# Attention and Mish feed-forward in one fp32 kernel: first k and v over 128 partitions, q loads and result stores on two DMA queues, a new order of the beginning

## The chip, the cores and the metric

One core of one Trainium2 chip. The metric is the time of one execution on the device in microseconds (us). The kernel before was run three times; the median counts.

## The reference, cut to what matters

```python
# q, k, v: (8, 8, 576, 64) fp32 = (batch, heads, seq, head_dim); g_norm: (64,)
kv  = einsum('bhsd,bhse->bhde', k, v)
out = einsum('bhsd,bhde->bhse', q, kv)
out = out / sqrt(mean(out * out, axis=-1) + 1e-6) * g_norm
x   = out.transpose(0, 2, 1, 3).reshape(4608, 512)
# moe_w_in: (512, 2048), moe_w_out: (2048, 512), handed over as float64
h   = x @ w_in
g   = h * tanh(log1p(exp(h)))       # Mish
y   = g @ w_out                     # (4608, 512) fp32
```

## The kernel before, in words

The 4608 tokens are worked in nine blocks `j` of 512. Part 1 makes, for each block, the linear attention, the norm and the first matrix product with Mish, and stores `g` to DRAM (`gd`). Part 2 reads `g` back and makes the second matrix product, in 18 groups of 256 tokens.

Both matrix products use a seven-product scheme in the manner of Strassen (the forms A11, S1, S2, A12, S4, S3, A22 of the left side against T1 to T4, B11, B21, B22 of the weights). Each fp32 operand is split into two fp32r halves: ACT casts the high half (L117), VectorE (DVE) subtracts to get the low half (L118). So ACT and DVE pass work to and fro all the time. One product of a form is 12 matmuls in part 1 (`mm_in`, L489) and is called a slot; a block `j` has 28 slots, with its group of four times seven products. Sums of products are taken from PSUM by ACT copies (L452, L457, L466) and DVE adds (L510). A bank `a` or `bc` is written a second time only after ACT has copied it.

The weights come as float64 words. `weight_forms` loads a block (1 MB in two DMAs, L133), ACT scales it (L138), DVE joins the halves of the words (L143 to L145) and makes differences (L153 to L155), and ACT and DVE split the forms (L117, L118). There are eight such blocks for `w_in`, made between the start and about slot 15.

The order is written by hand: straight code from L548 to L593 for the beginning, then tables of steps by slot (`at(t, ...)`). Within each engine instructions run in this order. SP issues all loads and stores of part 1 up to the last block, in order. Every DMA carries one of eight semaphores that are handed out in turn, and its issue waits until the DMA that carried the same semaphore before it has landed; so SP has at most eight DMAs under way, and a ninth issue waits for the first.

The beginning: `weights(0, LOAD)` loads the first weight block; `kv_first` (L214) loads k and v of batch 0, four heads at a time, into 64 partitions of nine rows each, and `kv_first_product` (L223) multiplies them, 36 matmuls for two pairs of heads. A unit `u` (0 or 1) is four heads of a block. `load` (L288) of a unit fetches q for 32 partitions per DMA, four DMAs where the block lies in one batch and eight where it lies in two. `transpose` (L300, DVE), `project` (PE), `square` (ACT, L339 for the second unit of block 0), `sums` (PE), `rstd` (ACT: Ln and Exp, L370 and L371), `normalize` (DVE, L392) follow. In later blocks the row of `rstd` is stored to DRAM (`keep`, `rd`) and read back to all partitions (`spread`, L386). The q tile `qs` has one buffer, so the load of the next unit waits for the transpose of the one before. The load of unit 1 of a block stands at slot 3 (block 1) and later six slots before the block's end, just behind `spread`; that of unit 0 stands some nineteen slots before its block begins.

The store of results is `o_store` (L731): for each group of 256 tokens four DMAs of 32 partitions (more where the group crosses a batch). In the first group of part 2 it follows a chain of DVE adds (L832 to L838).

Of the kernel before, what the change touches and what calls it, by code (L numbers as in the profile page):

```python
# [26 lines left out]
def linear_attention_rms_mish_ffn(  # L27
# [33 lines left out]
    nc = tc.nc  # L61
# [62 lines left out]
    def weight_forms(srcs, m, n, room, forms, put=None):  # L124
# [4 lines left out]

        def load():  # L130
            t = room()
            for src, places in srcs:
                nc.sync.dma_start(t[:, places].rearrange("p b (m n) t -> p (b m) (n t)", m=m), src)  # L133
            st["w"] = t.rearrange("p b n t -> p (b n) t")
# [78 lines left out]

    def kv_first(h0):  # L214

        ts = []
        for src in (k, v):
            t = wfp.tile([S // 9, 4, 9 * D], F32, name="wf")
            nc.sync.dma_start(t, src[0, h0:h0 + 4].rearrange("h (p c) d -> p h (c d)", c=9))
            ts.append(t)  # L220
        return ts

    def kv_first_product(h0, kt, vt):  # L223
        for i in range(2):
            for c in range(9):
                for o in range(2):
                    d = slice(c * D, (c + 1) * D)
                    nc.tensor.matmul(kvps[o * D:(o + 1) * D, 0, h0 // 2 + i, :], kt[:, 2 * i + o, d], vt[:, 2 * i + o, d], start=(c == 0), stop=(c == 8))

# [55 lines left out]
    def unit_steps(j, u):  # L285
        st = {}

        def load(t=None):  # L288


            t = qs[u] = att.tile([P, 2, T // R * D], F32, name="qs") if t is None else t
            for i in range(4):
                for b, s0, cols in segments(j):
                    run = (cols.stop - cols.start) // R * D
                    src = q[b, 4 * u + i // 2, s0:s0 + 1, R * (i % 2):]
                    src = bass.AP(src.tensor, src.offset, [[run, R], [2 * S * D, 2], [1, run - R]])
                    c0 = cols.start // R * D
                    nc.sync.dma_start(t[i * R:(i + 1) * R, :, c0:c0 + run - R], src)

        def transpose():  # L300
            t = att.tile([P, 2, T], F32, name="fh" if j < T32 else "fl")
# [245 lines left out]

    nc.scalar.preload_act_table_set("natural_log_exp_and_others")  # L548
# [182 lines left out]
    def o_store(st):  # L731

        i, half = divmod(st["s"], T // G)
        for n in range(P // R):
            c = (half * G + n * R) // R
            for b, s0, cols in segments(i):
                first, L = cols.start // R, (cols.stop - cols.start) // R
                rs = [r for r in range(2) if first <= c + r * P // R < first + L]
                if rs:
                    row = b * S + s0 + c + rs[0] * P // R - first  # L740
                    dst = out[row:row + 1, :]
                    dst = bass.AP(dst.tensor, dst.offset, [[L * DM, R], [P // R * DM, len(rs)], [1, DM]])
                    nc.sync.dma_start(dst, st["o"][n * R:(n + 1) * R, rs[0]:rs[-1] + 1, :])

# [147 lines left out]
```

## Time and profile before

| what | value |
|---|---|
| three runs, median (lowest to highest) | 893.97 us (893.43 to 894.04) |
| the profiled execution's own time | 892.98 us |
| its span in the trace | 891.2 us |
| granted TensorE clock, mean over the span | 0.986 |
| PE busy / DVE busy / ACT busy | 829.7 / 614.2 / 460.8 us |

The profiled execution lies 0.99 us under the median of the runs. In rows of the timeline the columns are the start, the duration, the engine, the source line, the operation, the output and inputs, the shape, the count, and in brackets the idle time of the engine before it with what ended it. SPq and ACTq are rows in which SP or ACT issues a DMA.

### The profile page before, as it was taken

The numbers are of one execution on the slowest core, as the hardware profiler recorded it, in microseconds if no ns is written. First come the engines' busy times: TensorE is split into PE (matmuls) and PEld (weight loads), VectorE is DVE, ScalarE is ACT, GpSimd is POOL, SyncE is SP. The second block draws the span as 40 slices with busy tenths as digits, with TensorE's granted clock in tenths as the row PEclk, the third lists the DMA queues.
The fourth block names the chain that finished last, engine by engine and source line by source line (L and its number), as shares of the span: only waits on it lengthen the run. The fifth ranks groups of instructions, "written<-read, shape, count | busy, mean of one in ns | idle before, by whom it ended". The sixth has DMA issues, their size and how long they took to land.

```text
span 891.2 us, 17127 instructions
## 1 busy us (share of the span) xinstructions
PE 829.7 (93%) x7004; PEld 796.6 (89%) x7004; DVE 614.2 (69%) x808; ACT 460.8 (52%) x698; POOL 4.3 (0%) x21
## 2 busy tenths in 40 slices
PE   1678899998999999999999899999999999999997
PEld 1366699897999999999899899999999999999997
DVE  3799676776777667777765358876766667777772
ACT  2565666565575666666675344434444443434431
POOL 1000000000000000000000000000000000000000
PEclk9988999999999999999999999999999999999999
DMA  9958698987979897777567995344443443334421
GB/s 224 277 135 255 179 287 243 252 255 236 291 225 295 244 240 223 210 218 199 215 180 242 420 420 170 118 120 149 153 146 121 133 129 119 118 119 131 155 71 48
DMA packets 154766, 177.42 MB, mean 199 GB/s; under 512 B 17408, under 2 KB 135168, under 8 KB 153664
## 3 DMA queue, kind: packets, MB, share of 16 engines
q1 hardware_dynamic: 151936, 172.13, 64.0%
q10 hardware_dynamic: 2752, 4.20, 1.2%
q8 instruction: 55, 0.90, 0.4%
q14 instruction: 23, 0.19, 0.1%
HBM read 114.30 MB, written 62.00 MB: 198 GB/s over the span
## 4 chain that ended last, share of the span: by engine, by line
PE 65%; DMA 10%; DVE 10%; ACT 8%; issue 4%; SPq 1%; ACTq 0%; DVEq 0%
PE a L720 21%; PE bc L720 16%; PE a L489 14%; PE bc L489 8%; DMA gd<-ula 4%; PE s L246 2%; DVE ur L510 1%; DMA wf<-in_v_dram 1%; DMA gd<-ur 1%; DMA w<-in_moe_w_in_dram 1%; DMA vm<-in_v_dram 1%; DVE gf L118 1%; ACT L374 1%; ACT gf L117 1%; ACT L114 1%
## 5 line engine op out<-in xcount | busy, mean ns | idle before, releaser
L720 PE MATMUL a<-wf,gf 128*128 128x256 f32 x1632 | 201.8, 283 | 0.5 <-DVE ur L751 0.5
L720 PEld LDWEIGHTS a<-wf,gf 128*128 128x128 f32 x1632 | 198.4, 192 | 0.7 <-DVE ur L751 0.7
L118 DVE TENSOR_TENSOR gf<-g,gf 128x1024 fp32r<-128x1024 f32 (+1 forms) x123 | 133.0, 1087 | 89.4 <-ACT gf L117 89.4
L489 PE MATMUL a<-gf,wf 128*128 128x256 f32 x1296 | 175.3, 289 | 10.1 <-ACT ur L466 4.7
L489 PEld LDWEIGHTS a<-gf,wf 128*128 128x128 f32 x1296 | 165.6, 196 | 17.2 <-ACT ur L466 7.1
L489 PE MATMUL bc<-gf,wf 128*128 128x256 f32 x1296 | 170.7, 285 | 3.5 <-ACT ur L457 2.4
L489 PEld LDWEIGHTS bc<-gf,wf 128*128 128x128 f32 x1296 | 161.7, 191 | 5.1 <-ACT ur L457 2.6
L117 ACT CAST gf<-g 128x1024 fp32r<-128x1024 f32 (+1 forms) x123 | 114.5, 939 | 93.4 <-DVE g L700 65.1
L720 PE MATMUL bc<-wf,gf 128*128 128x256 f32 x1224 | 152.7, 283 | 1.3 <-DVE gf L118 1.3
L720 PEld LDWEIGHTS bc<-wf,gf 128*128 128x128 f32 x1224 | 149.4, 192 | 1.7 <-ACT gf L117 1.0
L489 PE MATMUL a<-a,wf 128*128 128x256 f32 x432 | 60.0, 290 | 7.1 <-DVE ur L510 7.1
L489 PEld LDWEIGHTS a<-a,wf 128*128 128x128 f32 x432 | 56.1, 195 | 10.3 <-DVE ur L510 5.2
L114 ACT ACTIVATE ur<-ur 128x1024 f32<-128x1024 f32 x36 | 38.1, 1059 | 38.5 <-DVE ur L510 38.5
L118 DVE TENSOR_TENSOR fa<-fl,fh 128x1024 fp32r<-128x1024 f32 x28 | 34.2, 1223 | 19.6 <-ACT fh L117 18.6
L118 DVE TENSOR_TENSOR gf<-gf 128x512 fp32r<-128x512 f32 x45 | 30.3, 689 | 23.0 <-ACT gf L117 23.0
L117 ACT CAST gf<-a 128x1024 fp32r<-128x1024 f32 x17 | 17.9, 1052 | 53.3 <-DVE a L697 50.8
L457 ACT COPY ur<-bc 128x512 f32<-128x512 f32 (+1 forms) x53 | 27.4, 517 | 31.7 <-PE bc L720 23.0
L117 ACT CAST gf<-gf 128x512 fp32r<-128x512 f32 x45 | 27.1, 618 | 31.8 <-DVE gf L413 19.1
L466 ACT COPY ur<-a 128x512 f32<-128x512 f32 (+1 forms) x53 | 27.4, 516 | 30.3 <-PE a L720 24.6
L510 DVE TENSOR_TENSOR ula<-bc,ula 128x512 f32<-128x512 f32 x36 | 24.7, 687 | 26.1 <-PE bc L489 26.0
L114 ACT ACTIVATE ula<-ula 128x512 f32<-128x512 f32 x36 | 22.8, 633 | 22.1 <-DVE ula L510 22.0
L510 DVE TENSOR_TENSOR ur<-bc,ur 128x512 f32<-128x512 f32 x36 | 24.4, 678 | 11.3 <-PE bc L489 5.7
(128 smaller groups left out, 850.2 us busy)
## 6 DMA issues: line engine op xcount, KB each, us to landing
g<-gd SPq DMA_DIRECT2D x18, 2048.0 KB, 8.7
gd<-ur SPq DMA_DIRECT2D x32, 512.0 KB, 3.4
wod<-wst SPq DMA_DIRECT2D x16, 896.0 KB, 5.9
wf<-wod SPq DMA_DIRECT2D x8, 1792.0 KB, 17.1
gd<-ula SPq DMA_DIRECT2D x32, 256.0 KB, 5.4
gd<-ulb SPq DMA_DIRECT2D x32, 256.0 KB, 4.8
w<-in_moe_w_out_dram SPq DMA_DIRECT2D x32, 256.0 KB, 5.0
km<-in_k_dram SPq DMA_DIRECT2D x28, 256.0 KB, 4.5
```

The costliest lines, as they stand in the source:

```text
L114: nc.scalar.activation(o, i, AF.Mish)
L117: nc.scalar.copy(hi, src)
L118: nc.vector.tensor_sub(lo, src, hi.bitcast(F32))
L246: nc.tensor.matmul(kvps[o * D:(o + 1) * D, b % 2, h0 // 2 + i, :], kt, vt, start=(c == 0), stop=(c == CM))
L374: nc.scalar.preload_act_table_set("natural_log_exp_and_others")
L457: then(t + 2, lambda: nc.scalar.copy(dst(st, "22"), st["c"]))
L466: then(t + 4, lambda: nc.scalar.copy(dst(st, "12"), st["a"]))
L489: nc.tensor.matmul(bank[:, jj], w[:, right, a, kc, :], xf[:, b, kc, :], start=first and jj == kc == s == 0, stop=(kc == 1 and s == 2), ski ...
L510: nc.vector.tensor_add(o, bank, o)
L720: nc.tensor.matmul(bank, gf[:, a, c, :], wo[c][:, right, b, :], start=first and c == s == 0, stop=(c == NF2 - 1 and s == 2), skip_group_ch ...
```

## The change

Five things are edited.

1. `kv_first` and `kv_first_product`: k and v of batch 0 go to all 128 partitions, one head of a pair in partitions 0 to 63 and the other in 64 to 127. They are loaded in two pieces of two pairs of heads each. The matmuls of the two heads of a pair now read different halves of the partitions.
2. Every q load is divided: the DMAs for partitions 0 to 63 stay on SP, those for 64 to 127 are issued by ACT.
3. The same for the result stores of part 2.
4. The first weight block is loaded half by SP and half by ACT, and the preload of ACT's table stands behind these first DMAs.
5. The beginning has a new order: both q units are loaded before k and v, w block 0 is finished before k and v are multiplied, both transposes come early, and `rstd` of unit 0 and `project` of unit 1 are moved. The second unit of block 0 is transposed into spare room of its own tile.

```diff
-        def load():
+        def load(second=nc.sync):
             t = room()
-            for src, places in srcs:
-                nc.sync.dma_start(t[:, places].rearrange("p b (m n) t -> p (b m) (n t)", m=m), src)
+            for (src, places), eng in zip(srcs, (nc.sync, second)):
+                eng.dma_start(t[:, places].rearrange("p b (m n) t -> p (b m) (n t)", m=m), src)
...
+    kv0 = []
+
+    def kv_first(n):
+        for t, src in zip(kv0, (k, v)):
+            src = src[0, 2 * n.start:2 * n.start + 1]
+            src = bass.AP(src.tensor, src.offset, [[9 * D, P], [2 * S * D, n.stop - n.start], [1, 9 * D]])
+            nc.sync.dma_start(t[:, n], src)
+
+    def kv_first_product(n):
+        kt, vt = kv0
+        for hp in range(n.start, n.stop):
             for c in range(9):
                 for o in range(2):
-                    d = slice(c * D, (c + 1) * D)
-                    nc.tensor.matmul(kvps[o * D:(o + 1) * D, 0, h0 // 2 + i, :], kt[:, 2 * i + o, d], vt[:, 2 * i + o, d], start=(c == 0), stop=(c == 8))
+                    r, d = slice(o * D, (o + 1) * D), slice(c * D, (c + 1) * D)
+                    nc.tensor.matmul(kvps[r, 0, hp, :], kt[r, hp, d], vt[r, hp, d], start=(c == 0), stop=(c == 8))
...
-                    nc.sync.dma_start(t[i * R:(i + 1) * R, :, c0:c0 + run - R], src)
+                    (nc.sync if i < 2 else nc.scalar).dma_start(t[i * R:(i + 1) * R, :, c0:c0 + run - R], src)
...
-    nc.scalar.preload_act_table_set("natural_log_exp_and_others")
-    weights(0, LOAD)
-    kv0 = [kv_first(0)]
+    first, second = slice(0, 2), slice(2, NKC)
+    conv[0][LOAD](nc.scalar)
+    do(0, 0, "load")
+    t = wfp.tile([P, 3, 2 * T], F32, name="wf")
+    units[0][1]["load"]((t[:, 0:2], t[:, 2].rearrange("p (a t) -> p a t", a=2)))
+    kv0 += [wfp.tile([P, NKC, 9 * D], F32, name="wf") for _ in range(2)]
+    kv_first(first)
     weights(1, LOAD)
-    do(0, 0, "load")
-    kv0.append(kv_first(4))
-    units[0][1]["load"](wfp.tile([P, 2, T // R * D], F32, name="wf"))
+    kv_first(second)
...
+    nc.scalar.preload_act_table_set("natural_log_exp_and_others")
...
-    weights(0, SCALE, JOIN)
-    kv_first_product(0, *kv0[0])
-    kv_keep(0, slice(0, 2))
-    weights(0, DIFF, BLOCKS, SUMS)
+    weights(0, SCALE, JOIN, DIFF, BLOCKS)
+    do(0, 0, "transpose")
+    weights(0, SUMS)
+    do(0, 1, "transpose")
     weights(1, SCALE, JOIN)
-    do(0, 0, "transpose", "project")
-    weights(1, DIFF, BLOCKS, SUMS)
-    do(0, 0, "square")
-    kv_first_product(4, *kv0[1])
-    kv_keep(0, slice(2, 4))
+    kv_first_product(first)
+    kv_keep(0, first)
+    do(0, 0, "project", "square")
+    weights(1, DIFF, BLOCKS)
+    kv_first_product(second)
+    kv_keep(0, second)
     do(0, 0, "sums")
+    do(0, 1, "project")
+    weights(1, SUMS)
+    do(0, 0, "rstd")
     k_load(1, 0)
     k_load(1, 1)
     weights(4, LOAD)
     do(1, 0, "load")
-    do(0, 1, "transpose", "project")
-    do(0, 0, "rstd")
+    do(0, 1, "square", "sums")
     weights(2, SCALE)
-    do(0, 1, "square", "sums")
...
-                    nc.sync.dma_start(dst, st["o"][n * R:(n + 1) * R, rs[0]:rs[-1] + 1, :])
+                    (nc.sync if n < 2 else nc.scalar).dma_start(dst, st["o"][n * R:(n + 1) * R, rs[0]:rs[-1] + 1, :])
```

What this does to the order is shown at three places. The first is ACT in the beginning, between the Ln and Exp of block 0's unit 0 (`fa`) and what follows. `fl<-wf` is the scaling of weight block 2, `fh<-a` the squares of unit 1, `gf<-gf` the cast of form A11. In brackets are the semaphores that the instruction waits for; the DMAHW ones belong to DMAs. Before:

```order
L370 ACTIVATE fa<-bc,eps 128x512 [waits PE_49] x2
L371 ACTIVATE fa<-fa 128x1024 [waits Activation_49]
L138 ACTIVATE fl<-wf 128x1024 [waits DMAHW3_49,DMAHW2_49,DVE_49]
L339 ACTIVATE fh<-a 128x512 [waits DVE_49,PE_49]
L339 ACTIVATE fh<-a 128x512
L117 CAST gf<-gf 128x512 [waits DVE_49]
L370 ACTIVATE fh<-ss,eps 128x512 [waits PE_49]
```

Now, at the same place:

```order
L378 ACTIVATE fa<-bc,eps 128x512 [waits PE_49] x2
L379 ACTIVATE fa<-fa 128x1024 [waits Activation_49]
L304 DMA qs<-in_q_dram 32x2x96 [waits DMAHW4_49,DMAHW3_49,DMAHW2_49]
L304 DMA qs<-in_q_dram 32x2x864 [waits DMAHW5_49]
L304 DMA qs<-in_q_dram 32x2x96 [waits DMAHW6_49]
L304 DMA qs<-in_q_dram 32x2x864 [waits DMAHW7_49]
L347 ACTIVATE fh<-a 128x512 [waits PE_49] x2
L138 ACTIVATE fl<-wf 128x1024 [waits DMAHW3_49,DMAHW2_49,DVE_49]
L117 CAST gf<-gf 128x512 [waits DVE_49]
L378 ACTIVATE fh<-ss,eps 128x512 [waits PE_49]
```

Four q loads of block 1 stand ahead of the squares and of the scaling, and squares and scaling have changed places. SP's rows of the changed kernel tell whose semaphores these are (`w_329` is weight block 4, `vr` is the rest of v of batch 1):

```order
L210 DMA vr<-in_v_dram 64x2x64 [waits DMAHW5_49]
L133 DMA w_329<-in_moe_w_in_dram 128x4x256 [waits DMAHW6_49,DVE_49,Activation_49]
L133 DMA w_329<-in_moe_w_in_dram 128x4x256 [waits DMAHW7_49]
L304 DMA qs<-in_q_dram 32x2x96 [waits DMAHW0_49,DVE_49]
L304 DMA qs<-in_q_dram 32x2x864 [waits DMAHW1_49]
```

The two DMAs of weight block 4 carry semaphores 6 and 7, and ACT's third and fourth q load carry them next, so these two issues wait until block 4 has landed.

The second place is ACT at the load of unit 1 of a later block (here block 3), between the copies of banks `a` and `bc`. Before:

```order
L114 ACTIVATE ur<-ur 128x1024 [waits DVE_49]
L452 COPY ula<-a 128x512 [waits DMAHW1_49,PE_49]
L117 CAST wst<-w_1385 128x4x128 [waits DVE_49]
L457 COPY ur<-bc 128x2x256 [waits DMAHW3_49,PE_49]
L114 ACTIVATE ulb<-a 128x512 [waits DMAHW0_49,PE_49]
```

Now:

```order
L114 ACTIVATE ur<-ur 128x1024 [waits DVE_49]
L460 COPY ula<-a 128x512 [waits DMAHW1_49,PE_49]
L304 DMA qs<-in_q_dram 32x2x352 [waits DMAHW5_49,DMAHW4_49,DMAHW3_49]
L304 DMA qs<-in_q_dram 32x2x608 [waits DMAHW6_49]
L304 DMA qs<-in_q_dram 32x2x352 [waits DMAHW0_49]
L304 DMA qs<-in_q_dram 32x2x608 [waits DMAHW2_49]
L117 CAST wst<-w_1382 128x4x128 [waits DVE_49]
```

Four issues stand between the two copies. SP's rows at this place tell whose landings they wait for (`fh` and `fa` from `rd` are the four DMAs of `spread`, the second carrying semaphore 6 and the fourth semaphore 0; the first q load carries 2):

```order
L394 DMA fh<-rd_113 64x2x512 [waits DMAHW5_49,DMAHW4_49,PE_49]
L394 DMA fh<-rd_113 64x2x512 [waits DMAHW6_49]
L394 DMA fa<-rd_113 64x2x512 [waits DMAHW7_49]
L394 DMA fa<-rd_113 64x2x512 [waits DMAHW0_49]
L516 DMA gd_95<-ulb 128x2x256 [waits DMAHW1_49,Activation_49]
L304 DMA qs<-in_q_dram 32x2x352 [waits DMAHW2_49,DVE_49]
```

ACT's second and third q load wait until the second and the fourth DMA of `spread` have landed, the fourth until SP's first q load has landed; SP issues that one behind `spread`, and after DVE's transpose of the unit before.

The third place is ACT at the start of part 2, where the first group is stored; `q` is its PSUM, `ur` its result tile. Before:

```order
L831 COPY ur<-q_5860 128x256 [waits DMAHW5_49,PE_49]
L117 CAST gf<-g 128x1024 [waits PE_49,Activation_49]
L452 COPY ur<-a 128x256 [waits DMAHW2_49,PE_49]
L117 CAST gf<-g 128x1024 [waits DVE_49,Activation_49]
L457 COPY ur<-bc 128x256 [waits PE_49]
```

Now:

```order
L844 COPY ur<-q_5857 128x256 [waits DMAHW5_49,PE_49]
L756 DMA out_dram<-ur 32x2x512 [waits DVE_49]
L756 DMA out_dram<-ur 32x2x512 [waits DMAHW0_49]
L117 CAST gf<-g 128x1024 [waits PE_49,Activation_49]
L460 COPY ur<-a 128x256 [waits DMAHW2_49,PE_49]
L117 CAST gf<-g 128x1024 [waits DVE_49,Activation_49]
```

ACT's two stores wait for DVE's last add into the tile, and the cast and the copies of the next group stand behind them.

More of the change, by code (lines that the diff above doesn't have):

```diff
@@ L288, in load @@
         def load(t=None):
-            t = qs[u] = att.tile([P, 2, T // R * D], F32, name="qs") if t is None else t
+            if t is None:
+                t = att.tile([P, 2, T // R * D], F32, name="qs")
+            else:
+                t, st["qt"] = t
+            qs[u] = t
             for i in range(4):
@@ L297, in load @@
                     c0 = cols.start // R * D
-                    nc.sync.dma_start(t[i * R:(i + 1) * R, :, c0:c0 + run - R], src)
+                    (nc.sync if i < 2 else nc.scalar).dma_start(t[i * R:(i + 1) * R, :, c0:c0 + run - R], src)
         def transpose():
-            t = att.tile([P, 2, T], F32, name="fh" if j < T32 else "fl")
+            t = st.get("qt")
+            if t is None:
+                t = att.tile([P, 2, T], F32, name="fh" if j < T32 else "fl")
             src = qs[u].rearrange("p a (c d) -> p (a c) d", d=D)[:, :, 0:R]
```

9 lines of the change are left out of this document (removed).

## The prediction

> **What bounds the kernel now.** I read the busy times by stage first, then the beginning in the timeline, then the places where the change puts DMA issues into ACT's order. The stages (columns: stretch, its length, busy us and count for PE, weight loads, DVE, ACT, POOL, then granted clock, DMA share, GB/s):
>
> ```profile
> 0.00:42.00 42.00, 16.31 (x162) 10.01 (x163) 22.27 (x28) 16.71 (x24) 4.31 (x21) 1.00 0.99 247
> 300.00:350.00 50.00, 49.87 (x450) 47.60 (x449) 35.65 (x54) 32.45 (x51) 0.00 (x0) 1.00 0.87 255
> 554.00:883.00 329.00, 328.53 (x2736) 328.33 (x2736) 232.17 (x229) 135.79 (x178) 0.00 (x0) 1.00 0.40 122
> ```
>
> In the first 42 us the DMA engines are full (0.99) and PE, DVE and ACT mostly wait. In the middle of part 1 PE is full, and ACT still has 50.0 - 32.45 = 17.5 us of idle time in 50. In part 2 PE is full and ACT is idle for more than half. So a gain can come only from the first 42 us and the end, and a loss wherever ACT gets late enough to stop PE. How near that is, the list of PE's waits between 100 and 490 us tells:
>
> ```profile
> PE a L489 <- ACT ur L466: 4.7, 4, 2.0
> ```
>
> PE already stops for ACT's copy of bank `a`, for 4.7 us in four places, up to 2.0 us at once. ACT has idle time on the average, but at some copies none.
>
> How fast the first loads go, by form, is in three stretches. In the first mainly k and v of heads 0 to 3 land (64 partitions); in the second q (32 partitions each), the second half of k and v, and q again; in the third weight blocks 2 and 3 (128 partitions):
>
> ```profile
> 6.20:13.00 6.80, 0.00 (x0) 0.00 (x0) 4.69 (x6) 1.12 (x1) 0.00 (x0) 1.00 1.05 219
> 17.40:31.10 13.70, 5.60 (x60) 3.10 (x62) 10.13 (x13) 6.42 (x10) 0.00 (x0) 1.00 1.06 233
> 31.20:37.80 6.60, 4.95 (x30) 2.33 (x25) 3.50 (x5) 5.28 (x9) 0.00 (x0) 1.00 1.10 335
> ```
>
> Loads into part of the partitions run at 219 to 233 GB/s, loads into all of them at 335. That is what edits 1 and 2 aim at.
>
> The beginning as it is (first the two rows that belong to weight block 0, then DVE's longest wait, the first k and v product, and the chain around unit 1):
>
> ```profile
> 0.74 1.28 ACT L548 ACT_TABLE_LOAD   x1 [0.74 <-PEq L876]
> 6.23 1.12 ACT L138 ACTIVATE fl<-w 128x1024 f32<-128x1024 f32 x1 [4.21 <-DMA w<-in_moe_w_in_dram]
> 13.19 4.11 PE L228 MATMUL s<-wf 64*64 64x64 f32 x72 [13.19 <-DMA wf<-in_v_dram]
> 18.38 1.21 DVE L118 TENSOR_TENSOR wf<-fl,wf 128x256 fp32r<-128x256 f32 x2 [6.14 <-ACT wf L117]
> 35.38 1.11 ACT L138 ACTIVATE fl<-wf 128x1024 f32<-128x1024 f32 x1
> 36.39 1.07 ACT L339 ACTIVATE fh<-a 128x512 f32<-128x512 f32 x2
> 36.83 0.68 DVE L143 TENSOR_SCALAR fl<-fl 128x1024 uint32<-128x1024 uint32 x1
> 40.86 1.41 DVE L392 SCALAR_TENSOR_TENSOR gf<-a,gcol,fh 128x512 f32<-128x512 f32 x2 [0.22 <-ACT fh L371]
> 41.66 1.69 PE L489 MATMUL a<-gf,wf 128*128 128x256 f32 x12 [2.65 <-DVE gf L392]
> 44.93 0.31 SPq L298 DMA_DIRECT2D qs<-in_q_dram  x1
> ```
>
> The last row is SP's eighth q load of block 1. Its semaphore was that of the second half of weight block 4, so it marks when block 4 had landed: 44.93. The first product of part 1 starts at 41.66, so nothing before it waits for block 4 today.
>
> **The change part by part.**
>
> *The beginning: what is gained.* k and v of batch 0 are 2.36 MB, q of block 0 is 2.03 MB, 4.39 MB in all. At the mean of the two slow stretches, 226 GB/s, they take 19.4 us; at 335 they take 13.1. If the split does for q what 128 partitions do for the weights, everything behind them lands 6.3 us earlier, and block 4 at 38.6. DVE's wait of 6.14 us at 18.38 goes too, since weight block 0 is finished before k and v are multiplied; but DVE is then held by the landing of weight block 1. The scaling of block 0, which was at 6.23, comes later, as ACT's fourth q issue first waits for block 0's own half and the table load of 1.28 us stands behind that: some 1.7 us, covered by that 6.14 us of idle time. The k and v product runs on two halves of the rows; no row shows such a pair, so I bound it by nothing and by the 4.11 us of today. Either is covered: k and v land by some 20 us, and product, copies, projection and squares of unit 0 end near 34 us, before the event that comes next.
>
> *The beginning: what is lost.* ACT's third and fourth q load of block 1 wait for weight block 4, and the squares of unit 1 and the scaling of block 2 now stand behind them. With block 4 at 38.6 and one issue of 0.43 us (the pace of two DMA issues of ACT in a row, below) ACT comes free at 39.0. Two squares (1.07) end at 40.1, the scaling (1.11) at 41.2; DVE's join of block 2, at 36.83 today, starts at 41.2, the subtraction behind it at 44.3, the normalization at 45.0 instead of 40.86. The first product follows it: **4.2 us later.** If the loads don't get faster at all, block 4 lands at 44.9 and the loss is 10.5 us; at the 420 GB/s that the page's slices of 22.28 us show once (slices 23 and 24) the 4.39 MB take 10.5 us, block 4 lands at 36.0, and it is 1.6:
>
> ```profile
> GB/s 224 277 135 255 179 287 243 252 255 236 291 225 295 244 240 223 210 218 199 215 180 242 420 420 170 118 120 149 153 146 121 133 129 119 118 119 131 155 71 48
> ```
>
> *q of block 1, unit 1, and block 2, unit 0.* The first row pair shows the pace of ACT's issues; then scaling and join of block 4; then what stands around the load of block 2:
>
> ```profile
> 530.44 0.34 ACTq L516 DMA_DIRECT2D gd<-ur  x1
> 530.87 0.39 ACTq L508 DMA_DIRECT2D gd<-ulb  x1
> 60.30 1.15 ACT L138 ACTIVATE fl<-w 128x1024 f32<-128x1024 f32 x1
> 61.48 0.69 DVE L143 TENSOR_SCALAR fl<-fl 128x1024 uint32<-128x1024 uint32 x1
> 79.62 0.59 ACT L114 ACTIVATE ulb<-a 128x512 f32<-128x512 f32 x1
> 80.35 1.15 ACT L138 ACTIVATE fl<-w 128x1024 f32<-128x1024 f32 x1
> 81.47 0.37 SPq L516 DMA_DIRECT2D gd<-ur  x1
> ```
>
> Four issues take 1.7 us. At 59 us a cast of about 1 us runs while the first are issued, so the scaling at 60.30 and the join at 61.48 come **0.9 us** later (0 to 1.7). At 79 us ACT's fourth issue waits for the landing of SP's first q load of the same unit; today SP's store at 81.47 carries that load's semaphore next, so it lands by 81.4. ACT issues at 81.4, is free at 81.85, does Mish (0.59) and scales block 6 at 82.45 instead of 80.35: **2.1 us** (0 to 2.5). Blocks 4 to 7 hang one on the other through one buffer (load, scale, join, load), so these delays reach slot 21, where block 7 is needed.
>
> *q of block 2, unit 1.* ACT's copy of `bc`, SP's last v load of that stretch, PE's product behind the copy, and how long such a load takes (KB each, median us to landing):
>
> ```profile
> 111.59 0.59 ACT L457 COPY ur<-bc 128x512 f32<-128x512 f32 x1
> 113.39 0.37 SPq L209 DMA_DIRECT2D vm<-in_v_dram  x1
> 113.47 3.04 PE L489 MATMUL bc<-gf,wf 128*128 128x256 f32 x24
> vm<-in_v_dram SPq DMA_DIRECT2D x28, 256.0 KB, 4.3
> ```
>
> ACT's fourth issue waits for that v load (113.39 + 4.3 = 117.7) and the copy for the issue: 118.1 instead of 111.59. The second half of the PE row, from 114.91 on, needs the copy; PE stops until 118.7, 3.8 us. With some of it made up I take **3.0 us** (0 to 6.5).
>
> *q of blocks 3 to 8.* One block in the middle (SP's eight q issues, ACT's copies of `bc` and `a`, PE's product behind the latter, time to landing of such q loads):
>
> ```profile
> 318.12 4.67 SPq L298 DMA_DIRECT2D qs<-in_q_dram  x8
> 320.13 0.59 ACT L457 COPY ur<-bc 128x512 f32<-128x512 f32 x1
> 322.14 0.59 ACT L466 COPY ur<-a 128x512 f32<-128x512 f32 x1 [0.34 <-PE a L489]
> 324.82 3.04 PE L489 MATMUL a<-gf,wf 128*128 128x256 f32 x24
> qs<-in_q_dram SPq DMA_DIRECT2D x16, 120.0 KB, 4.2
> ```
>
> SP's first q load, on which ACT's fourth waits, lands at 318.12 + 4.2 = 322.3; the copy at 320.13 moves to 322.7, by 2.6 us, and that at 322.14, behind Mish and a cast, to 324.5. It ends at 325.1, 0.3 us after PE wanted it. Unit 0's load costs ACT its four issues, 1.7 us less about 0.5 beneath the operation that runs: 1.2. So ACT loses 3.8 us a block. Directly PE loses 0.3; the rest lies beside 17.5 us of idle time, but comes at the casts and copies that DVE and PE wait for. I take 1.2 us a block, a third, times six: **7.2 us** (0 to 6 x 3.8 = 22.8).
>
> *Stores.* At the start of part 2 (ACT's copy of bank `a`, PE's product that needs it, DVE's last add, PE's next wait):
>
> ```profile
> 545.67 0.37 ACT L452 COPY ur<-a 128x256 f32<-128x256 f32 x1
> 546.52 3.04 PE L720 MATMUL a<-wf,gf 128*128 128x256 f32 x24
> 548.36 0.41 DVE L838 TENSOR_TENSOR ur<-q,ur 128x256 f32<-128x256 f32 x1
> 553.98 2.27 PE L720 MATMUL bc<-wf,gf 128*128 128x256 f32 x17 [0.83 <-DVE gf L118]
> 886.62 0.32 SPq L743 DMA_DIRECT2D out_dram<-ur  x1
> 887.92 0.43 SPq L743 DMA_DIRECT2D out_dram<-ur  x1
> ```
>
> ACT's two stores wait for the add (548.77) and take 0.86 us; then a cast, and the copy at 550.7 instead of 545.67. PE starts that product at 551.1 instead of 546.52, 4.6 us late; the waits that PE had behind it (0.83 us, and some of the one before) give part back: **3.0 us** (0 to 4.7), and behind it PE is full to the end. The other stores follow ACT's own copies and lie in its idle time. At the end the four issues were 886.62 to 887.92, two and two end with the second, 0.9 us earlier: **-0.9 us.**
>
> Sum: 4.2 + 0.9 + 2.1 + 3.0 + 7.2 + 3.0 - 0.9 = 19.5 us. On the profiled execution's 892.98 that is 912.5 us; the median of the runs lies 1.0 above the profiled one, and 19.5 on it is 913.5. I take 913.
>
> **The rivals.**
>
> *A, ACT's idle time takes most of it.* If ACT's waits in part 1 after block 2 and at part 2's start are absorbed, 4.2 + 0.9 + 2.1 + 1 - 0.9 = 7.3 stay: 900 us. For it speak the 17.5 us of idle time in 50; against it the 4.7 us for which PE already waits for the copy.
>
> *B, all of it reaches PE.* 4.2 + 0.9 + 2.1 + 6.5 + 22.8 + 4.7 - 0.9 = 40 us, 933 us. Against it: a third of ACT's time is free, and DVE's too.
>
> *C, the halves don't help.* Both queues run over the same DMA engines, already 0.99 busy; then q stays at 233 GB/s and only k and v gain, 2.36 MB from 10.8 us (219) to 7.0 (335). Block 4 lands at 44.93 - 3.8 = 41.1, the beginning costs 6.7 instead of 4.2, and the time is 915 us. The Trainium skill says this in "DMA: Bandwidth & Descriptors", section "Rules for kernel authors": two transfers to disjoint halves of the partitions aren't worth making, since they share the same engines and serialize. The rows of 219 and 335 GB/s speak against full equality, since the number of partitions does count here; two queues at once are in no row.
>
> *D, faster.* The first 10.8 MB (q, k, v of batch 0, weight blocks 0 to 4, and four heads of batch 1) land at 420 GB/s from 2 us on, block 4 by 28 us, before ACT reaches the q load (Exp of unit 0 near 34). Then the wait disappears, the removed 6.14 us at 18.38 counts, and if the rest is as in A without its 4.2 the time is 892.98 - 6.1 + 3.1 = 890 us. It decides when block 4 lands before 34.8 us, 10 us earlier than today; 6.3 are worked out.
>
> **How the numbers follow.** Forecast 0.50, C 0.12, A 0.18, B 0.10, D 0.10. The predicted time is the forecast's, 913 us. The range reaches down to A's 900 less the 3 us of the loads of blocks 1 and 2, if those are hidden too (897), and up to the forecast with a beginning that costs 10.5 instead of 4.2 and another 0.7 us in each of blocks 3 to 8 (913 + 6.3 + 4.2, some 924). It leaves out B and D, 2 in 10. About 0.2%, 1.8 us, is what a measurement can tell from no change. D and the lowest end of A give faster 0.07 and same 0.04; slower 0.89.
>
> **What would show it.** In the changed profile the beginning is right if ACT sits behind the q issues of block 1 until block 4 has landed, and the first product starts at 45 to 47 instead of 41.66. It is wrong if that product starts before 41. The rate is right if the stretch of q, k and v runs over 300 GB/s. Blocks 3 to 8 are right if PE gets waits for ACT's L465 and L474 (copies of `bc` and `a`) behind each unit 1 load and the period of a block grows by 1 to 2 us; wrong if PE stays full there. Part 2's start is right if PE waits some 3 to 5 us for the copy L460. The prediction falls if ACT's issues show no wait, or if PE's idle time in 100 to 490 us doesn't grow.

## The result, and the profile after

| | before | after |
|---|---|---|
| median of four runs (lowest to highest) | 893.70 us (892.35 to 894.04) | 923.86 us (923.53 to 924.25) |
| span of the profiled execution | 891.2 us | 921.7 us |
| granted TensorE clock, mean | 0.986 | 0.979 |
| PE / DVE / ACT busy | 829.7 / 614.2 / 460.8 us | 836.9 / 612.7 / 460.6 us |

The change makes the kernel slower: the ratio is 1.0341, 95% interval 1.0327 to 1.0355. That is 30 us, of which the prediction had 19.5. The measured time stands at the very end of its range, which went to some 924 us; 1.0341 times the 893.97 us that the prediction started from is 924.5.

DVE and ACT are busy as long as before. What is new is when they are. First the beginning of the changed kernel by stretches (columns as in the prediction: stretch, length, busy us of PE, weight loads, DVE, ACT, POOL, granted clock, DMA share, GB/s):

```profile
6.20:13.00 6.80, 0.00 (x0) 0.00 (x0) 2.65 (x3) 2.40 (x2) 0.00 (x0) 1.00 1.02 279
13.00:20.00 7.00, 2.25 (x42) 2.28 (x44) 6.39 (x9) 1.97 (x3) 0.00 (x0) 1.00 1.06 337
20.00:26.00 6.00, 5.28 (x92) 3.88 (x90) 3.96 (x5) 3.09 (x6) 0.00 (x0) 1.00 1.08 362
```

Where 219 and 233 GB/s were, there are now 279 (mostly q of block 0) and 337 (mostly k and v). The transfers did get faster. Then the timeline of ACT, DVE and PE behind them (ACT's four issues, and the last of them by itself):

```profile
34.55 4.36 ACTq L304 DMA_DIRECT2D qs<-in_q_dram  x4
38.59 0.32 ACTq L304 DMA_DIRECT2D qs<-in_q_dram  x1
38.95 0.60 ACT L347 ACTIVATE fh<-a 128x512 f32<-128x512 f32 x1 [8.15 <-DMA qs<-in_q_dram]
44.88 1.41 DVE L400 SCALAR_TENSOR_TENSOR gf<-a,gcol,fh 128x512 f32<-128x512 f32 x2
45.68 0.59 PE L497 MATMUL a<-gf,wf 128*128 128x256 f32 x2 [2.65 <-DVE gf L400]
```

ACT's fourth q issue of block 1 goes out at 38.59, when weight block 4 has landed (38.6 was predicted). The squares of unit 1 follow at 38.95, after 8.15 us in which ACT ran nothing, and the first product starts at 45.68 instead of 41.66.

In part 1 PE's waits from block 3 on (148 to 520 us) have doubled: the list adds up to 19.1 us, and in the same part of the kernel before (137 to 494 us) to 9.1. Its four longest (us in total, times, longest):

```profile
PE a L497 <- ACT ur L474: 7.0, 7, 1.6
PE a L497 <- ACT ula L460: 4.5, 3, 2.1
PE bc L497 <- ACT ur L465: 3.0, 2, 1.7
PE ss L371 <- DVE fa L118: 2.5, 4, 0.9
...
```

The waits for ACT's copies are those the prediction named. To see where each microsecond went, I matched the matmuls of the two traces one by one, the k-th of L489 with the k-th of L497 and in part 2 those of L720 with those of L733:

| place | starts before | starts after | behind by |
|---|---|---|---|
| first product of part 1 | 41.66 | 45.68 | 4.0 |
| behind q of block 2, unit 0 | 109.15 | 117.23 | 8.1 |
| behind q of block 2, unit 1 | 124.81 | 134.86 | 10.05 |
| behind q of blocks 3 to 7, just ahead of that of block 8 | 390.27 | 416.00 | 25.7 |
| part 2, ahead of the first stores | 542.21 | 567.84 | 25.6 |
| part 2, behind the first stores | 556.93 | 587.72 | 30.8 |
| end of the span | 891.2 | 921.7 | 30.5 |

Half of the loss lies in blocks 3 to 8; the loads of block 8 add nothing to it. PE's listed waits grow by 10.0 us in this part, the lag by 15.6: another 1.7 us is TensorE's clock (last section), and the rest stands in no row of the waits. One load there, that of block 6 unit 0, in the timeline (SP's four issues, ACT's last two, ACT's last one by itself, the copy behind it, then three later rows):

```profile
314.02 1.95 SPq L304 DMA_DIRECT2D qs<-in_q_dram  x4
316.06 3.01 ACTq L304 DMA_DIRECT2D qs<-in_q_dram  x2
318.76 0.32 ACTq L304 DMA_DIRECT2D qs<-in_q_dram  x1
319.12 0.58 ACT L465 COPY ur<-bc 128x512 f32<-128x512 f32 x1 [2.33 <-DMA qs<-in_q_dram]
320.31 0.43 DVE L143 TENSOR_SCALAR wx<-wx 128x512 uint32<-128x512 uint32 x1 [2.26 <-ACT wx L138]
329.84 1.06 ACT L114 ACTIVATE ur<-ur 128x1024 f32<-128x1024 f32 x1 [1.95 <-DVE ur L518]
337.52 3.14 PE L497 MATMUL a<-gf,wf 128*128 128x256 f32 x24 [1.41 <-ACT ur L474]
```

ACT's fourth issue waits until SP's first q load of the same unit has landed, 4.7 us after SP issued it; ACT runs nothing for 2.33 us, and the copy of `bc` stands behind that. DVE in turn waits 2.26 us for what ACT scales next. Eighteen microseconds after that copy PE waits 1.41 us for a copy that is still late.

At part 2's start, and at the end of the kernel (timeline):

```profile
574.42 0.86 ACTq L756 DMA_DIRECT2D out_dram<-ur  x2
575.38 1.04 ACT L117 CAST gf<-g 128x1024 fp32r<-128x1024 f32 x1 [4.95 <-DVE ur L851]
576.33 0.36 ACT L460 COPY ur<-a 128x256 f32<-128x256 f32 x1
576.75 5.38 PE L733 MATMUL a<-wf,gf 128*128 128x256 f32 x24 [4.43 <-ACT ur L460]
...
917.01 0.37 ACT L761 COPY ur<-a 128x256 f32<-128x256 f32 x1 [10.38 <-PE a L733]
917.40 0.79 SPq L756 DMA_DIRECT2D out_dram<-ur  x2
917.41 0.85 ACTq L756 DMA_DIRECT2D out_dram<-ur  x2
```

ACT waits 4.95 us with its stores for DVE's last add, and a cast and the copy of bank `a` stand behind them. The product that took 3.04 us before now takes 5.38.

### The profile page after: what moved, and what is told of

Read it like the earlier page. It is cut to its first block, busy times and chain, and to the rows that moved or that the text cites. A ratio compares the mean times of both kernels' runs of the same rounds, so it can differ in the third digit from the quotient of the medians.

```text
span 921.7 us, 17059 instructions
## 1 busy us (share of the span) xinstructions
PE 836.9 (91%) x7004; PEld 800.1 (87%) x7004; DVE 612.7 (66%) x808; ACT 460.6 (50%) x698; POOL 4.3 (0%) x21
## 4 chain that ended last, share of the span: by engine, by line
PE 51%; DMA 17%; DVE 13%; ACT 11%; issue 5%; SPq 2%; ACTq 1%; DVEq 0%
PE a L733 21%; PE bc L733 16%; PE a L497 7%; DMA qs<-in_q_dram 6%; PE bc L497 5%; DMA gd<-ula 4%; DVE ur L518 2%; DMA wod<-wst 1%; DMA fa<-rd 1%; ACT gf L117 1%; DMA wf<-in_q_dram 1%; PE s L248 1%; DVE fa L118 1%; DMA wf<-in_k_dram 1%; DVE gf L350 1%
## 5 line engine op out<-in xcount | busy, mean ns | idle before, releaser
L733 PE MATMUL a<-wf,gf 128*128 128x256 f32 x1632 | 204.1, 285 | 4.9 <-ACT ur L460 4.4
L733 PEld LDWEIGHTS a<-wf,gf 128*128 128x128 f32 x1632 | 200.6, 194 | 5.4 <-ACT ur L460 4.6
L497 PE MATMUL a<-gf,wf 128*128 128x256 f32 x1296 | 174.4, 288 | 15.1 <-ACT ur L474 7.2
L497 PE MATMUL bc<-gf,wf 128*128 128x256 f32 x1296 | 174.8, 288 | 10.2 <-ACT ur L465 6.9
L497 PEld LDWEIGHTS a<-gf,wf 128*128 128x128 f32 x1296 | 163.3, 193 | 23.3 <-ACT ur L474 9.6
L497 PEld LDWEIGHTS bc<-gf,wf 128*128 128x128 f32 x1296 | 164.7, 194 | 13.3 <-ACT ur L465 8.0
L733 PE MATMUL bc<-wf,gf 128*128 128x256 f32 x1224 | 152.4, 283 | 0.0
L733 PEld LDWEIGHTS bc<-wf,gf 128*128 128x128 f32 x1224 | 149.3, 192 | 0.0
L497 PE MATMUL a<-a,wf 128*128 128x256 f32 x432 | 60.6, 291 | 6.4 <-DVE ur L518 6.4
L497 PEld LDWEIGHTS a<-a,wf 128*128 128x128 f32 x432 | 56.6, 197 | 10.6 <-DVE ur L518 5.5
L114 ACT ACTIVATE ur<-ur 128x1024 f32<-128x1024 f32 x36 | 38.1, 1058 | 37.8 <-DVE ur L518 37.8
L117 ACT CAST gf<-gf 128x512 fp32r<-128x512 f32 x45 | 27.1, 619 | 33.4 <-DVE gf L421 19.1
L474 ACT COPY ur<-a 128x512 f32<-128x512 f32 (+1 forms) x53 | 27.4, 516 | 28.8 <-PE a L733 25.4
L114 ACT ACTIVATE ula<-ula 128x512 f32<-128x512 f32 x36 | 22.8, 634 | 22.1 <-DVE ula L518 22.1
```

The costliest lines, as they stand in the source:

```text
L114: nc.scalar.activation(o, i, AF.Mish)
L117: nc.scalar.copy(hi, src)
L474: then(t + 4, lambda: nc.scalar.copy(dst(st, "12"), st["a"]))
L497: nc.tensor.matmul(bank[:, jj], w[:, right, a, kc, :], xf[:, b, kc, :], start=first and jj == kc == s == 0, stop=(kc == 1 and s == 2), ski ...
L733: nc.tensor.matmul(bank, gf[:, a, c, :], wo[c][:, right, b, :], start=first and c == s == 0, stop=(c == NF2 - 1 and s == 2), skip_group_ch ...
```

## The experiments

The theory from these rows: ACT's DMA issues wait for semaphores that SP's transfers hold, ACT stands still meanwhile, and its copies and casts come late (theory W). The first four kernels undo parts of the change. In every kernel of this section the computation is complete. Ratios are to runs of the kernel before on the same chip. Kernels 1 to 4, 5 to 8, and 9 and 10 ran on three chips, on which the kernel before took 895.35, 893.73 and 892.63 us; so a difference of 3 us between kernels of two groups is not certain by the times alone, and the matched matmuls of the traces are given beside it.

**1. q of blocks 2 to 8 back on SP's queue.**

```diff
-  (nc.sync if i < 2 else nc.scalar).dma_start(t[i * R:(i + 1) * R, ...
+  (nc.sync if i < 2 or j >= 2 else nc.scalar).dma_start(t[i * R:(i + 1) * R, ...
```

> The q loads of blocks 2 to 8 go back to SP's queue alone; the new beginning, the divided loads of blocks 0 and 1 and the divided stores stay. Theory W (ACT sits at its own q issues of blocks 2 to 8, and PE waits for what ACT copies and casts behind them): the steps by which PE falls behind in the changed kernel's trace go, 4.0 us at the load of block 2 unit 0, 2.0 at unit 1, 15.6 at blocks 3 to 8: 923.9 - 21.6 = 902 us, between 900 and 905. Rival L (the late beginning is handed on: the weight blocks come late and the pipeline behind them never recovers, whoever issues q): most of the 21.6 us stays, 918 to 924 us.

Measured: 901.3 us, ratio 1.0075 (1.0046 to 1.0105). Theory W holds, rival L falls. In its trace PE is 5.3 us behind the kernel before at 109.15 and 4.7 at the end of part 1: a late beginning is handed on, but does not grow. So the beginning with block 1 costs 5.3 of the 8.1 in the table, and q of block 2, unit 0, the other 2.8.

**2. SP's half one slot later.** The load is divided into two steps: ACT's half stays in its slot, and SP's half follows in the next (blocks 2 to 8).

```diff
-  (0, 8 - NS if j > 2 else 9 - NS, "load"), ... (1, 22 - NS, "load"),
+  (0, 8 - NS if j > 2 else 9 - NS, "load_act"), (0, 9 - NS if j > 2 else 10 - NS, "load_sp"),
+  ... (1, 22 - NS, "load_act"), (1, 23 - NS, "load_sp"),
```

> As the changed kernel, but for blocks 2 to 8 SP issues its half of a q load one slot (about 3 us) after ACT's half. ACT still makes all its four issues per load, at the same place, but the semaphores that its fourth one needs are no longer those of SP's half of the same load. Theory W-wait (the waits at the issues are what costs): of some 20 us that ACT waits at these issues most goes and so does most of PE's loss of 21.6 us; 904 to 912 us. Rival W-issue (the four issues themselves, 1.7 us a load, are what costs): 920 to 924 us.

Measured: 936.8 us, ratio 1.0473 (1.0440 to 1.0506). Both expectations missed, since the edit did not remove the waits. The semaphores passed to other transfers of SP (stores of weights and of `gd`, the spread), some of which land later still. At block 7 ACT's fourth issue waits for a store of weights that SP issued at 399.95 us, and goes out at 408.95 (timeline: ACT's last two issues, the copy, PE's next weight load):

```profile
403.69 5.58 ACTq L304 DMA_DIRECT2D qs<-in_q_dram  x2
409.36 0.59 ACT L471 COPY ur<-bc 128x512 f32<-128x512 f32 x1 [6.24 <-DMA qs<-in_q_dram]
410.00 0.29 PEld L503 LDWEIGHTS bc<-gf,wf 128*128 128x128 f32 x1 [3.79 <-ACT ur L471]
```

With as many issues as the changed kernel, and longer waits at them, the kernel loses 13 us more. That speaks against W-issue; experiment 5 takes away the waits in another way.

**3. The stores back on SP's queue.**

```diff
-  (nc.sync if n < 2 else nc.scalar).dma_start(dst, ...
+  nc.sync.dma_start(dst, ...
```

> All result stores go back to SP's queue; everything else as in the changed kernel. Theory S (at part 2's start ACT's cast and copy stand behind its two stores, which wait for the last add): PE's 5.1 us at that place go, the end loses the 0.3 us that it had gained: 923.9 - 4.8 = 919.1 us. Rival: PE's wait there comes from weights and forms that are late since part 1, and moves to another wait: 923 to 924 us.

Measured: 918.7 us, ratio 1.0272 (1.0241 to 1.0302), as theory S has it. In its timeline the copy of bank `a` and the product are no longer behind the stores:

```profile
571.48 0.37 ACT L460 COPY ur<-a 128x256 f32<-128x256 f32 x1
572.35 3.04 PE L733 MATMUL a<-wf,gf 128*128 128x256 f32 x24
574.62 1.77 SPq L756 DMA_DIRECT2D out_dram<-ur  x4
```

**4. Only the beginning.** The edits of experiments 1 and 3 together, with `j >= 1` in place of `j >= 2`: what stays is k and v in 128 partitions, the new order, and weight block 0 and q of block 0 on two queues.

> Only the beginning of the change is kept: k and v of batch 0 in 128 partitions, the new order, and q of block 0 (with weight block 0) divided between two queues. All q loads of blocks 1 to 8 and all stores are SP's. Theory W: ACT no longer waits 8.2 us for weight block 4, the squares of unit 1 run at about 31 us, the first product of part 1 starts 2 to 4 us before the 41.66 of the kernel before, and nothing is lost later: 888 to 891 us. Rival (the faster loads are worth nothing, since the weights behind the first product set the pace): 893 to 894 us.

Measured: 888.6 us, ratio 0.9928 (0.9901 to 0.9955): faster than the kernel before. The squares of unit 1 no longer wait (timeline):

```profile
30.50 1.07 ACT L347 ACTIVATE fh<-a 128x512 f32<-128x512 f32 x2
37.17 2.55 PE L497 MATMUL a<-gf,wf 128*128 128x256 f32 x12 [4.05 <-DVE gf L400]
```

They run at 30.50 instead of 38.95, the first product starts at 37.17, 4.5 us before that of the kernel before, and at the end of part 1 PE is still 4.4 us ahead.

**5. Half the issues, hardly any wait.**

```diff
+  (nc.scalar if i == 3 or j < 2 and i == 2 else nc.sync).dma_start(t[i * R:(i + 1) * R, ...
```

> For blocks 2 to 8 ACT issues only the last quarter of a q load (two issues where the changed kernel has four), SP the rest; all else as in the changed kernel. In this program the second of the two issues waits for a transfer made well before the load (of k, or the first spread of the roots), no longer for one of the load itself, so ACT keeps half the issues and hardly any wait. Theory W-wait (the 20 us that ACT waits at the issues are the cost): most of PE's 21.6 us goes, 902 to 906 us. Rival W-issue (the issues themselves): half of the 21.6 us stays, 912 to 914 us. If the waits at the spread stay as long as the 2 to 3 us of the load of unit 1 in the changed kernel: over 915 us.

Measured: 904.6 us, ratio 1.0114 (1.0091 to 1.0137). The load of block 6 unit 0 again, in this kernel's timeline (ACT's two issues, and what it runs between and behind them):

```profile
303.62 0.34 ACTq L304 DMA_DIRECT2D qs<-in_q_dram  x1
303.88 1.05 ACT L117 CAST fh<-fl 128x1024 fp32r<-128x1024 f32 x1
303.99 0.44 ACTq L304 DMA_DIRECT2D qs<-in_q_dram  x1
304.84 0.59 ACT L465 COPY ur<-bc 128x512 f32<-128x512 f32 x1
```

Both issues pass beside a cast, and the copy follows at once. What ACT loses at the q issues can be measured: these kernels and kernel 1 run the same 698 instructions on ACT in the same order. So each one's lateness against kernel 1 can be taken, and what it grows by from the instruction ahead of a load's first issue to the one behind its last. For blocks 2 to 8, added up, with the time above kernel 1 by the medians and by the matched matmuls:

| kernel | issues | ACT falls behind at them | time | above kernel 1 | in the traces |
|---|---|---|---|---|---|
| 1, all on SP | 0 | 0 | 901.3 us | 0 | 0 |
| 5, a quarter on ACT | 26 | 3.3 us | 904.6 us | 3.3 us | 5.7 us |
| the change | 52 | 25.2 us | 923.9 us | 22.6 us | 21.6 us |
| 2, SP's half later | 52 | 34.8 us | 936.8 us | 35.5 us | 33.8 us |

Kernel 5's profiled execution, at 908.1 us, is the slowest of its four. The changed kernel's list of ACT's waits in 75 to 500 us has nearly the same sum, 25.4 us in nine waits:

```profile
ACT ur L465 <- DMA qs<-in_q_dram: 16.0, 6, 4.3
ACT wst L117 <- DMA qs<-in_q_dram: 7.1, 2, 3.8
ACT ulb L114 <- DMA qs<-in_q_dram: 2.3, 1, 2.3
```

The other five of these fourteen loads (unit 0 of blocks 3, 4 and 7, and both of block 8) have their issues on ACT as well, but these need not wait, and ACT runs on without a gap. The issues themselves take 9.5 us in kernel 5 and 18.7 in the change, most of it beside operations that run. So the loss goes with the waits and not with the number of issues: theory W-wait. In its trace kernel 5 loses 2.4 us more than ACT does at its issues; the cause of these is open.

**6. POOL's queue instead of ACT's**, on kernel 4, for blocks 1 to 8.

```diff
+  (nc.sync if i < 2 else (nc.scalar if j == 0 else nc.gpsimd)).dma_start(t[i * R:(i + 1) * R, ...
```

> As the kernel with only block 0 divided (888.6 us), but for blocks 1 to 8 the second half of each q load goes through POOL's queue instead of SP's; POOL has nothing else to do, and its issues wait only for the transpose that frees the buffer. Stores are SP's. Theory W (what costs is that ACT stands still, not that a load is divided): no loss, 887 to 890 us. Rival Q (two queues for one load make q or the transfers beside it land later, and that costs): 893 us or more.

Measured: 892.5 us, ratio 0.9982 (0.9966 to 0.9997): between the two theories, some 4 us over kernel 4 (5.7 in the traces). One cause is in its timeline (SP's issues of weight blocks, POOL's of q of block 1, PE's product of the second half of k and v):

```profile
15.77 5.83 SPq L133 DMA_DIRECT2D wf<-in_moe_w_in_dram  x4
17.34 2.24 POOL L304 DMA_DIRECT2D qs<-in_q_dram  x4 [11.98 <-DMA wf<-in_v_dram]
25.91 3.24 PE L230 MATMUL s<-wf 64*64 64x64 f32 x72 [2.10 <-DMA wf<-in_v_dram]
```

POOL has nothing else to do and issues its half of block 1 as soon as the transpose has freed the buffer (it ends at 17.04), while the second half of k and v and the weight blocks, which are needed earlier, are still under way. PE's product of that half waits 2.10 us for v and starts at 25.91, in kernel 4 at 24.25; the first product of part 1 starts at 40.08 instead of 37.17. The rest comes in small steps through part 1, and its cause stays open. Dividing the loads of blocks 1 to 8 costs some 4 us with POOL, where ACT's copies don't stand behind the issues.

**7. q of block 0 on SP's queue alone**, on kernel 4.

> As the kernel with only block 0 divided, but with q of block 0 on SP's queue alone too (only half of weight block 0 stays on ACT's). Theory H (the halves on two queues land faster: 279 GB/s in the stretch where 219 and 233 were had with one queue): q of block 0, 2.03 MB, takes 1.4 us longer and SP issues four more behind one another; weight blocks and first product come 1.5 to 3 us later, 890 to 891.5 us. Rival C (two queues share the same engines, so dividing is worth nothing; the gain is all the 128 partitions of k and v and the order): 888 to 889 us.

Measured: 891.8 us, ratio 0.9975 (0.9962 to 0.9988), just above the range of theory H and well above that of rival C. In the traces the first product starts 3.0 us later than in kernel 4, of which 1.4 are left at the end. The same stretch of this kernel, and then of kernel 4:

```profile
6.20:14.00 7.80, 0.00 (x0) 0.00 (x0) 5.06 (x8) 2.38 (x4) 0.00 (x0) 1.00 1.04 223
```

```profile
6.20:14.00 7.80, 0.00 (x0) 0.00 (x0) 3.76 (x4) 3.02 (x4) 0.00 (x0) 1.00 1.04 269
```

In both it is mainly q of block 0 that lands here: at 269 GB/s through two queues and at 223 through one, with the DMA engines as full in both (1.04). The Trainium skill ("DMA: Bandwidth & Descriptors", section "Rules for kernel authors") holds that two transfers to disjoint halves of the partitions are not worth making, as they share the engines, and advises one transfer over 128 partitions instead. That one was not run here. For these loads of 32 partitions each the measurement differs: a fifth more through two queues.

**8. Kernel 4 with the stores divided, except in part 2's first group.**

```diff
+  (nc.sync if n < 2 or st["s"] == 0 else nc.scalar).dma_start(dst, ...
```

> As the kernel with only block 0 divided, and the stores of all groups but part 2's first divided between SP and ACT. Theory S (the store cost lies at the first group alone, where the stores wait for DVE's last add; all later ones follow ACT's own copy): 0.3 us less than that kernel, 888.3 us. Rival (each of the 17 other pairs of stores costs PE something, as 5.1 us at the first): 890 us or more.

Measured: 888.8 us, ratio 0.9941 (0.9924 to 0.9959). The other 17 groups cost nothing that can be seen: by the matched matmuls this kernel is 0.78 us behind kernel 4 at the start of part 2 and 0.79 at its end. The 0.3 us at the end can't be seen either. The cost of the stores is the first group's alone.

**9 and 10. ACT's time by itself.** The question left was why so much of ACT's loss reaches PE. Kernel 4 gets needless table loads at the place of the q loads of blocks 3 to 8, one at the step and one that the next activation then needs.

```diff
         def load(t=None):
+            if j >= 3:
+                nc.scalar.preload_act_table_set("natural_log_exp_and_others")
```

> The kernel with only block 0 divided (888.6 us), with two needless loads of an activation table on ACT at each q load of blocks 3 to 8: 24 of them, 1.28 us each in the profile of before, 30.7 us in all, and no transfer, no issue and no semaphore more. In the changed kernel ACT stood 27.9 us at its q issues of these blocks and PE fell 15.6 us behind, 0.56 of it. Theory K (ACT's idle time is a wait for DVE in a chain that ACT itself feeds, so what ACT loses comes out at PE for more than half): 0.56 x 30.7 = 17 us, 906 us, between 902 and 910. Rival T (a third of it, as the prediction took): 10 us, 898 to 899 us. Rival D (ACT's time is harmless and the loss comes from q or its neighbours landing late): 888 to 891 us.

> As the kernel with 24 table loads, but only at the loads of unit 1: 12 table loads, 15.4 us of ACT's time. Theory K: the share depends on the place; the table loads fall around slot 22, where ACT in the changed kernel stood 19.1 us and PE fell 9.0 us behind (0.47): 7 us, 895 to 897 us. Rival T (a third everywhere): 5 us, 893 to 894 us. Rival D: 888 to 891 us.

Measured: 905.7 us, ratio 1.0141 (1.0102 to 1.0180), with all of them; 898.3 us, ratio 1.0055 (1.0040 to 1.0070), with those at unit 1 alone. Kernel 9's groups and PE's longest waits in 133 to 510 us:

```profile
L114 ACT ACT_TABLE_LOAD x21 | 26.9, 1283 | 0.4
L292 ACT ACT_TABLE_LOAD x12 | 15.4, 1283 | 0.2
```

```profile
PE a L497 <- ACT ur L474: 12.0, 11, 1.6
PE a L497 <- ACT ula L460: 3.3, 4, 0.9
```

Kernel 4 has 9 table loads at L114 and none at L292, so 24 x 1.283 = 30.8 us of ACT were added, and no transfer. The time grows by 17.1 us, 0.56 of it; in the traces PE falls 15.1 us behind kernel 4, 0.49. PE waits for the same copies as in the changed kernel (in kernel 4 these two rows are 2.8 and 2.6 us). At unit 1 alone it is 9.7 of 15.4 us, 0.63 (9.3 in the traces, 0.60), somewhat more than theory K had. Rival T falls, and rival D falls as the whole cause: ACT's time alone makes such a loss, and about half of it or more comes through.

The 27.9 and 19.1 us of ACT in these two expectations are too high as a measure of the issues: at the issues of blocks 3 to 8 ACT stands 18.8 us, 14.5 of them at unit 1 (from the list under experiment 5, less the 2.3 and 4.3 us of block 2). So the agreement of 0.56 with the changed kernel is chance; the next section has the share.

## Why the prediction was right in kind and short in size

| term | predicted | measured |
|---|---|---|
| beginning and q of block 1 | 4.2 + 0.9 | 5.3 |
| q of block 2 | 2.1 + 3.0 | 2.8 + 2.0 |
| q of blocks 3 to 8 | 7.2 | 15.6 |
| start of part 2 | 3.0 | 5.1 |
| end | -0.9 | -0.3 |
| sum | 19.5 | 30.5 |

**The beginning** came as worked out: block 4 at 38.6, the first product 4.0 us late. The rate of q was taken too high (335; the trace shows 279), that of the weights behind it too low (335; 362 in 20 to 26 us), and that the two made up for each other is luck. Rival C's ground fell in experiment 7. Rival D's gain is real, but only in kernel 4, where ACT has no q load of block 1 to issue; the changed kernel's wait for block 4 takes more than it.

**Blocks 1 and 2** were right in the sum, 6.0 us predicted, 10.05 - 4.0 = 6.05 measured, but the two loads of block 2 are each off by a third, in opposite directions; that the sum fits is luck too.

**Blocks 3 to 8** are the step that failed: "I take 1.2 us a block, a third, times six." PE fell 15.6 us behind there, 2.6 a block.

What ACT loses was not set too low: 3.8 x 6 = 22.8 us was assumed, 18.8 measured. At unit 1 it is 14.5 us, where 15.6 were assumed. At unit 0 it is 4.3 instead of 7.2, and not for the reason given. The prediction let that load cost its issues alone; issues that need not wait cost ACT nothing (blocks 3, 4, 7 and 8), and in blocks 5 and 6 the fourth issue waits for SP's first q load, so that ACT stands 1.95 and 2.33 us. The prediction had found this wait for block 2 and did not carry it on.

What failed is the share: 15.6 / 18.8 = 0.83 goes with ACT's waits, not a third. Not all of the 15.6 need be ACT's: 1.7 us is the clock (two stretches at half of it in blocks 3 and 4, where the kernel before has one), and in experiment 6, with no issue on ACT, divided loads cost 2.0 us in the same part (the trace is 3.9 us behind kernel 4 at its start and 5.9 at its end). Without these two it is 11.9 of 18.8, 0.63 (an estimate), near the 0.49 and 0.60 of experiments 9 and 10, in which no DMA was added or moved. How much of the two belongs here is not shown, but without both the share is still well over a third.

The argument was that ACT has 17.5 us of idle time in 50. Look at what that idle time is: the activation of `ur` behind the load of block 6, in the kernel before; its counterpart is the row of 329.84 above:

```profile
306.98 1.06 ACT L114 ACTIVATE ur<-ur 128x1024 f32<-128x1024 f32 x1 [1.95 <-DVE ur L510]
```

Before, ACT idles 1.95 us ahead of it, waiting for DVE. After, it idles 1.95 us as well, though everything is late by 2.3 us more than PE. DVE was late too, since it waits for what ACT scales and casts (the 2.26 us above). Here the idle time was moved, not used up: it lies inside a chain from ACT to DVE and back. The row shows one place; that it is so at most places is an inference from it and from the share.

Another weakness was to take one block for six. By the matched matmuls, from the start of one load to that of the next, unit 0 and unit 1 cost 1.3 and 3.0 us in block 3, 1.2 and 2.8 in block 4, 2.0 and 0.3 in block 5, 2.3 and 0.7 in block 6, 0 and 2.2 in block 7, and nothing in block 8 (a wait of ACT can come out at PE behind the next load's start). The one that the prediction shows, block 6 at unit 1, is among the cheapest.

**The start of part 2**: the copy was predicted at 550.7, and 576.33 less the 25.63 us that PE was behind there is 550.70; the product starts 4.6 us late as predicted. What was missed is the clock. In the stretch around this product TensorE ran at half of it:

```profile
575.00:581.80 6.80, 5.05 (x23) 5.05 (x24) 4.14 (x4) 3.58 (x5) 0.00 (x0) 0.50 0.26 77
```

The product takes 5.38 instead of 3.04 us, 2.3 more, and 1.8 are given back behind it: 4.6 + 2.3 - 1.8 = 5.1.

**The end**: the two queues end their issues 0.9 us earlier behind the last copy, as worked out, but the execution ends only 0.3 earlier. What follows the last issue became longer by the rest; the runs don't show why.

Rival A (the idle time takes most of it) was the error of the forecast in a larger dose. Rival B had the right places, but not all of ACT's time comes through, and ACT loses less than it took.

## What to carry to other kernels

In this program an engine that computes pays for a DMA issue with the time until the issue's semaphore is free, and everything behind it on that engine pays too; an issue that need not wait cost ACT next to nothing. Before moving an issue there, look up for each one which transfer it waits for and when that lands. Idle time of an engine is slack only if it waits for something that it doesn't feed itself: where two engines pass work to and fro, reckon with half of a delay or more at the end of the chain, and measure it by adding plain work at the place. Here the good part is the beginning alone (888.6 us, 0.7% under the kernel before), where loads into few partitions go through two queues ahead of all other work of ACT.

## What the runs showed of the hardware

In the kernel before and in the changed one TensorE's clock fell to half in stretches of 3.4 or 6.8 us (apart from one at the very end). Each began during a wait of PE of 1.74 us or more or within 1.2 us of its end: in the changed kernel at 182.5 us after a wait of 1.74 us, and at 575.0 in the wait of 4.43 us in part 2. After waits of 1.4 to 1.6 us there was none. Not every longer wait had one: the same wait of 2.4 us just before part 2 was followed by such a stretch in the kernel before, and by none in the changed one. This window holds the one at 182.5:

```profile
182.50:185.90 3.40, 3.40 (x17) 3.29 (x16) 3.02 (x4) 2.19 (x4) 0.00 (x0) 0.50 1.04 311
```

Half the clock for 3.4 us makes such a wait 1.7 us dearer. Where the wait falls in time decides as well: in each trace these stretches start on a grid of 3.41 us. The wait of 2.4 us lies within one field of the grid in the kernel before (first row, PE busy for 1.05 us), and is split between two in the changed one:

```profile
511.05:514.47 3.42, 1.05 (x9) 0.96 (x9) 0.69 (x1) 1.59 (x4) 0.00 (x0) 1.00 1.02 432
534.07:537.48 3.41, 2.43 (x21) 2.23 (x19) 0.69 (x1) 0.00 (x0) 0.00 (x0) 1.00 1.06 447
537.48:540.89 3.41, 2.03 (x17) 2.03 (x18) 0.24 (x1) 2.46 (x5) 0.00 (x0) 1.00 1.00 422
```

From where the two traces' records of the clock begin (29.8 and 22.1 us), every field at full clock with 2.0 us or more of idle time of PE was followed by half the clock, none with 1.73 us or less, and of the three between (1.74, 1.82 and 1.90 us) one. The Trainium skill ("TensorE: Matmul & The Clock Gate", section "Part 1: The HAM clock gate (the "warmup" mystery)") ties the half clock to an idle window of about 3.4 us; the length of the stretches agrees, but here about half a field of idle time was enough.

Two DMA queues moved loads of 32 partitions a fifth faster than one (269 against 223 GB/s), and an idle queue (POOL's) ran ahead of the order in which the data was needed (its q loads were issued from 17.34 us on, and the first product came 2.9 us later).
